# Gated linear attention and a soft mixture of experts: scores as sixteen 64x64 products, one DRAM row for k, q and v, more buffers, another order

## The chip, the core and the metric

The kernel runs on one core of a Trainium2 chip, in float32. The metric is the device time of one execution in microseconds. TensorE (PE) does the matrix products and transposes, with its weight loads shown as an engine of their own (PEld); VectorE (DVE), ScalarE (ACT) and GpSimd (POOL) do elementwise work; SyncE (SP) issues the DMAs.

## What is computed

Four batches of 768 tokens pass a linear attention of 8 heads of 48 columns with a gate per key column, and the result, 3072 tokens of 384 columns, passes a soft mixture of 8 experts with 4 slots each:

```python
f = 1 / (1 + exp(-f_logit))
for t in range(768):                                   # B=4, H=8, D=48
    state = f[:, :, t, :, None] * state + einsum('bhd,bhe->bhde', k[:, :, t], v[:, :, t])
    y[:, :, t] = einsum('bhd,bhde->bhe', q[:, :, t], state)
x = y.transpose(0, 2, 1, 3).reshape(3072, 384)
logits = x @ phi                                       # 384 x 32
d = softmax(logits, axis 0);  slot_input = d.T @ x
slot_out[e] = relu(slot_input[e] @ w1[e]) @ w2[e]      # 384 x 1024, 1024 x 384
out = softmax(logits, axis 1) @ slot_out
```

## The kernel before

**Blocks.** The attention is cut into 24 blocks of 128 tokens, six of each batch, in an order that walks the four batches side by side: block n belongs to batch n mod 4 and needs the state that block n-4 left. A block holds all eight heads as four pairs (a), each pair as two halves (r) of the 128 partitions, 48 rows used of 64. The two pairs of a bank are laid out in opposite directions of time, which is why masks and slices come mirrored.

In a block the gates come first: f is loaded (two blocks at a time), ACT takes exp and ln (L495, L498), DVE sums along time with two scans (L487, L488, with the tile `chain` of ones), and ACT takes exp of the sum and of its negative (L501, L502). Then k is multiplied by the one and q by the other (L524, L527, named mk and mq, on DVE or POOL). PE transposes k (L532, tk), a copy brings it from PSUM (L535, pk), PE forms k times v (L553, kv), and DVE adds the old state and scales it (L557, L562, sa and sm). For the output, PE multiplies q with the old state (L572, ie, not in the first four blocks), forms the scores of k with q (L541, sc), DVE multiplies them with a triangular mask (L544), PE multiplies them with v on top of the same bank (L581, ia), a copy brings the result to SBUF (L584, py), PE transposes it (L612, tx), and a copy makes it x (L615, px).

**Units.** After every fourth block a unit takes four blocks of x: logits (L630), running maximum, exponentials, their transposes (L651, L655), and a running sum of slot inputs (L659, L663). **The tail** after the last unit forms the slot inputs, runs the experts (first products L788 with twelve 1 MB tiles of w1, relu, transposes L803, second products L822 with twelve 1 MB tiles of w2), and combines and stores the output (L845, L854).

**The scores.** Each of a block's eight products takes 48 rows of k as weights, 128 columns wide, and streams 128 columns of q; the products of the two halves (r) use the two row halves of the array. The quarter of each 128x128 result that lies wholly above the diagonal is computed and masked out.

```python
for a in range(PR):
    for r in range(2):
        nc.tensor.matmul(ps[:, r, a], k_[rows[r], col(a)], queries(r, a), start=True, stop=True)
```

**What sets the order.** No order is written by hand. A class `Plan` takes every operation with its engine or choice of engines, the regions it reads and writes, a planned duration and a priority, and lists them greedily into one program order with a model of the engines. A table `LATER` shifts the priority of each kind of operation (eight numbers: blocks 0 to 3, then by block mod 4), a table `ENGINE` fixes the engine of a kind where there is a choice, and `WINDOW` says how near two starts must be for the priority to decide. The model counts a change of tile shape on PE, a page of 256 PE instructions to be fetched, and at most eight DMAs under way on SP's queue. Operations of POOL and those of DVE with two inputs in SBUF (scans, mk, mq) are made to exclude one another: each waits for the one before it in the program order. Each engine then runs its list strictly in order.

**Buffers.** k, q and v have rings of four blocks each (tiles ak, aq, av), scores two buffers (as), the gates three buffers of two blocks for f (af, ag) and two for the sums (ac). Of PSUM, one pair of banks (pr0) is the scores', two pairs (pr1, pr2) are y's, and two single banks (sg0, sg1) serve the rest. PE starts with 32 products of the tile `ones` with itself (L426), which warm it up; they wait for `ones` (L384), and DVE's first memsets clear banks (L403) and fill `chain` (L395).

Of the kernel before, what the change touches and what calls it, by code (L numbers as in the profile page):

```python
# [34 lines left out]
NHOME = 15  # L35
# [44 lines left out]
WINDOW = 0.21  # L80
LATER = {
# [1014 lines left out]
```

## Time and profile before

| | |
|---|---|
| median of 3 runs | 166.01 us (165.46 to 166.28) |
| the profiled execution | 165.66 us, of which the span from first to last instruction is 163.9 us |
| mean granted TensorE clock | 0.978 |
| PE busy | 146.5 us of the span (89%), 2461 matrix products |
| DVE busy | 120.2 us (73%) |
| ACT busy | 99.0 us (60%) |
| POOL busy | 26.3 us (16%) |
| DMA | 54.01 MB, 330 GB/s over the span |

The shares are averages over stages: a start up to about 28 us in which the first blocks' data arrive, the loop over the blocks up to about 113 us, the experts up to about 147 us, and the output. In the loop PE is busy nearly without a break, and DVE nearly so. A row of the chain of waits has a start, a duration and what ran then; rows of groups have a count, the busy time, the mean duration of one in ns, and the idle time of the engine before them with what ended it.

### The profile page before, as it was taken

The page shows a single profiled execution, that of the slowest core. Times are in us where ns is not written, and L with a number is a line of the kernel's source. Part 1 is how long each engine was busy: PE and PEld are TensorE (multiplying, and loading weights), DVE is VectorE, ACT ScalarE, POOL GpSimd, SP SyncE. Part 2 cuts the span into 40 slices and gives each one's busy share as a digit, 9 for nine tenths or more (in the row PEclk, how much of TensorE's full clock was granted, in tenths as well). Part 3 has the DMA queues.
Part 4 walks back from the last instruction along what each step waited for, and adds up shares of the span by engine and source line. Part 5 has one row for each costly group of instructions (what it writes and reads, how often), then busy time and mean ns, then how long its engine had stood idle before and what let it go on. Part 6 is the DMA issues. An engine that isn't in the chain of part 4 may idle for free.

```text
span 163.9 us, 5869 instructions
## 1 busy us (share of the span) xinstructions
PE 146.5 (89%) x2461; PEld 111.4 (68%) x2461; DVE 120.2 (73%) x234; ACT 99.0 (60%) x186; POOL 26.3 (16%) x43
## 2 busy tenths in 40 slices
PE   2978999999999999999999999999989999999500
PEld 2957777688777796788877887787852358677300
DVE  6789989899999999999999999999370133350400
ACT  4989987787869798873985876824430121033600
POOL 4002011050306030060308231250020000000000
PEclk9999999999999999999999999999999999999965
DMA  4999999999999899999999979529999996059491
GB/s 160 329 408 382 406 418 401 385 381 419 392 362 386 266 398 362 390 331 332 398 409 366 350 245 268 226 34 404 430 420 424 422 416 286 4 202 353 187 387 48
DMA packets 17603, 54.01 MB, mean 330 GB/s; under 512 B 1952, under 2 KB 5152, under 8 KB 14496
## 3 DMA queue, kind: packets, MB, share of 16 engines
q1 hardware_dynamic: 17568, 53.55, 86.2%
q8 instruction: 21, 0.34, 0.9%
q14 instruction: 14, 0.11, 0.2%
HBM read 48.82 MB, written 4.72 MB: 327 GB/s over the span
## 4 chain that ended last, share of the span: by engine, by line
PE 58%; DVE 13%; DMA 11%; ACT 9%; issue 3%; SPq 2%; POOL 1%; ACTq 0%; DVEq 0%; POOLq 0%
PE pr L541 10%; PE pr L581 6%; PE sg L612 5%; PE pr L788 5%; PE pr L572 5%; PE sg L822 5%; DMA av<-in_v_dram 5%; DMA ak<-in_k_dram 4%; DVE as L544 4%; PE sg L630 3%; PE pr L845 3%; PE sg L532 3%; PE sg L659 2%; DMA aq<-in_q_dram 2%; PE sg L553 2%
## 5 line engine op out<-in xcount | busy, mean ns | idle before, releaser
L544 DVE TENSOR_TENSOR as<-pr,tri 128x1024 f32<-128x1024 f32 x24 | 29.2, 1215 | 1.7 <-PE pr L541 1.0
L541 PE MATMUL pr<-aq,ak 48*128 48x128 f32 x384 | 27.9, 285 | 0.8 <-DVE ak L524 0.3
L541 PEld LDWEIGHTS pr<-aq,ak 48*128 48x128 f32 x384 | 23.3, 187 | 5.5 <-issue 2.4
L581 PE MATMUL pr<-as,av 128*48 128x128 f32 x384 | 24.1, 274 | 1.4 <-DVE as L544 1.2
L581 PEld LDWEIGHTS pr<-as,av 128*48 128x48 f32 x384 | 20.2, 123 | 3.0 <-DVE as L544 2.3
L612 PE MATMUL sg<-ident,xT 128*128 128x128 f32 x96 | 15.2, 282 | 0.4 <-ACT ag L535 0.2
L527 POOL TENSOR_TENSOR aq<-aq,ac 128x512 f32<-128x512 f32 x9 | 11.4, 1283 | 25.0 <-DMA aq<-in_q_dram 8.7
L584 ACT COPY xT<-pr 128x512 f32<-128x512 f32 x20 | 11.5, 582 | 5.5 <-PE pr L581 5.4
L524 POOL TENSOR_TENSOR ak<-ak,af 128x512 f32<-128x512 f32 x6 | 7.7, 1281 | 35.1 <-ACT af L501 23.4
L572 PE MATMUL pr<-aq,st 48*48 48x128 f32 x320 | 13.1, 279 | 0.2 <-DVE aq L527 0.2
L502 ACT ACTIVATE ac<-ac 128x1024 f32<-128x1024 f32 (+1 forms) x13 | 12.9, 993 | 0.5
L612 PEld LDWEIGHTS sg<-ident,xT 128*128 128x128 f32 x96 | 10.4, 141 | 3.6 <-issue 1.5
L532 PE MATMUL sg<-ident,ak 128*128 128x128 f32 x80 | 12.1, 282 | 0.2 <-DVE ak L524 0.2
L854 ACT COPY hm<-pr 128x768 f32<-128x768 f32 x7 | 5.5, 803 | 11.0 <-PE pr L845 11.0
L487 DVE TENSOR_TENSOR_SCAN ac<-chain,af 128x256 f32<-128x256 f32 x16 | 10.9, 683 | 1.1 <-issue 1.1
L535 ACT COPY ag<-sg 128x512 f32<-128x512 f32 x17 | 9.4, 585 | 3.6 <-PE sg L532 3.6
L615 ACT COPY xr<-sg 128x384 f32<-128x384 f32 x17 | 8.1, 480 | 4.9 <-PE sg L612 4.8
L488 DVE TENSOR_TENSOR_SCAN ac<-chain,af 128x256 f32<-128x256 f32 x16 | 10.7, 667 | 0.0
L553 PEld LDWEIGHTS sg<-av,ag 128*48 128x48 f32 x320 | 8.6, 124 | 2.7 <-issue 1.3
L527 DVE TENSOR_TENSOR aq<-aq,ac 128x512 f32<-128x512 f32 x15 | 10.2, 685 | 0.4 <-POOL ak L524 0.2
L572 PEld LDWEIGHTS pr<-aq,st 48*48 48x48 f32 x320 | 8.0, 119 | 3.4 <-issue 2.0
L532 PEld LDWEIGHTS sg<-ident,ak 128*128 128x128 f32 x80 | 8.5, 141 | 2.6 <-issue 0.9
(142 smaller groups left out, 240.7 us busy)
## 6 DMA issues: line engine op xcount, KB each, us to landing
hm<-in_w_dram SPq DMA_DIRECT2D x17, 1024.0 KB, 8.2
ak<-in_k_dram SPq DMA_DIRECT2D x24, 256.0 KB, 6.1
aq<-in_q_dram SPq DMA_DIRECT2D x24, 256.0 KB, 6.1
av<-in_v_dram SPq DMA_DIRECT2D x24, 192.0 KB, 5.6
out_dram<-hm SPq DMA_DIRECT2D x12, 384.0 KB, 3.8
af<-in_f_dram SPq DMA_DIRECT2D x7, 512.0 KB, 6.0
ag<-in_f_dram SPq DMA_DIRECT2D x4, 512.0 KB, 6.0
af<-in_w_dram SPq DMA_DIRECT2D x1, 1024.0 KB, 6.6
```

Source lines behind the costliest of these rows:

```text
L487: nc.vector.tensor_tensor_scan(cx[:, : 2 * BT], chain, lx[:, : 2 * BT], 0.0, op0=ALU.mult, op1=ALU.add)
L488: nc.vector.tensor_tensor_scan(cx[:, 2 * BT :][:, ::-1], chain, lx[:, 2 * BT :], 0.0, op0=ALU.mult, op1=ALU.add)
L502: add(f"p{n}", {"ACT": t_act(w)}, lambda e: nc.scalar.activation(flat(c_), flat(c_), AF.Exp, scale=-1.0), w=cs, prio=T(n, 1.2))
L527: tt(e)(flat(q_), flat(q_), flat(c_), op=ALU.mult)
L532: nc.tensor.transpose(pk[:, a], k_[:, a], ident)
L541: nc.tensor.matmul(ps[:, r, a], k_[rows[r], col(a)], queries(r, a), start=True, stop=True)
L544: tt(e)(sc_.rearrange("p r (m x) t -> p (r m) (x t)", x=2), bank(("sc", n)).rearrange("p r (m t) -> p (r m) t", m=2), tri.rearrange("p x t ...
L553: nc.tensor.matmul(pk[rows[r], col(a)], kp_[:, col(a), rows[r]], v_[:, 2 * a + r], start=True, stop=True)
L572: nc.tensor.matmul(py[at : at + D, r, a // 2], s0[rows[r], col(a)], queries(r, a), start=a < 2, stop=False, skip_group_check=True)
L581: nc.tensor.matmul(py[at : at + D, r, a // 2], v_[:, 2 * a + r], sc_[:, r, a], start=first and a < 2, stop=a >= 2, skip_group_check=True)
L584: copy(e)(xT[:, n % NXT].rearrange("p (r m) t -> p r (m t)", r=2), bank(("y", n))[:, :, : 2 * BT])
L612: nc.tensor.transpose(px[:, i], xT[:, n % NXT, i], ident)
```

## The change

**Scores.** A block's scores become sixteen products on the four 64x64 quadrants of the array (L588). For each pair and half, the 64 keys that all 128 queries may reach take 128 columns, and the other 64 keys only the 64 queries behind them. The skipped quarter of the bank is never written, so two memsets clear it at the start (L420).

**Inputs.** k, q and v of a block lie in one DRAM row of 1408 columns. Blocks 0 and 1 load three pieces, blocks 2 and 3 two (k with q, then v), the rest one; a ring of five blocks in one tile (ab) takes the place of ak, aq and av. The tiles of w1 are loaded in halves, spread over the blocks.

**Buffers.** Three score buffers, four for f, three for the sums; small tiles move to make room, and 13 tiles instead of 15 are kept for weights.

**Block 0.** Its gates and its products on k and q are done in two halves of two pairs.

**The order.** All numbers of `LATER`, the engines in `ENGINE`, `WINDOW` and some constants of the planner are new, the tail's groups stay the same, and the order of nearly everything moves. What each engine runs:

DVE at the start of the program, before: memsets, then the scans (L487, L488) and the products on q and k (L527, L524) of blocks 0 and 1, then block 0's mask (L544).

```order
L384 MEMSET ones 128x128
L409 COPY same<-ident 32x128 x4
L487 SCALAR_TENSOR_TENSOR ac<-chain,af 128x256
L488 SCALAR_TENSOR_TENSOR ac<-chain,af 128x256
L487 SCALAR_TENSOR_TENSOR ac<-chain,af 128x256
L488 SCALAR_TENSOR_TENSOR ac<-chain,af 128x256
L527 TENSOR_TENSOR aq<-aq,ac 128x512
L524 TENSOR_TENSOR ak<-ak,af 128x512
L527 TENSOR_TENSOR aq<-aq,ac 128x512
L524 TENSOR_TENSOR ak<-ak,af 128x512
L544 TENSOR_TENSOR as<-pr_62,tri 128x1024
```

(sg are the single banks, pr the pairs, ac and af tiles of the gates, tri the mask.) And now (st is a state), from the memset of `ones`, which stands behind those of pr0 and `chain`: block 0's halved scans (L522) and products (L571), the copy of its turned k (L579), its mask (L591), the scans of blocks 1 to 3 and block 0's state (L609), then block 1's product on k.

```order
L398 MEMSET ones 128x128
L426 COPY same<-ident 32x128 x4
L522 SCALAR_TENSOR_TENSOR ac<-chain,af 128x256 x2
L571 TENSOR_TENSOR ab<-ab,af 128x256 x2
L571 TENSOR_TENSOR ab<-ab,ac 128x256 x2
L579 COPY ag<-sg_65 128x512
L591 TENSOR_TENSOR as<-pr_62,tri 128x1024
L509 SCALAR_TENSOR_TENSOR ac<-chain,af 128x256
L510 SCALAR_TENSOR_TENSOR ac<-chain,af 128x256
L609 TENSOR_TENSOR st_86<-sg_66,ac 128x192
```

Block 1's products moved from before block 0's mask to behind it and behind six scans, and the copy of turned k, which ACT did, is now DVE's.

POOL from its triangular mask on, before: products on k (L524) and q (L527).

```order
L389 AFFINE_SELECT tri<-ones 128x128 x2
L524 TENSOR_TENSOR ak<-ak,af 128x512
L524 TENSOR_TENSOR ak<-ak,ag 128x512
L527 TENSOR_TENSOR aq<-aq,ac 128x512
L524 TENSOR_TENSOR ak<-ak,af 128x512 x2
```

And now (L571 is both products; those with ac or ae beside ab are q's of blocks 1 and 2, then of later ones):

```order
L403 AFFINE_SELECT tri<-ones 128x128 x2
L571 TENSOR_TENSOR ab<-ab,ac 128x512 x2
L534 COPY pend<-ac 128x8
L571 TENSOR_TENSOR ab<-ab,af 128x512
L571 TENSOR_TENSOR ab<-ab,ag 128x512 x2
L571 TENSOR_TENSOR ab<-ab,ae 128x512 x2
```

Up to block 4's mask POOL had two such products and has seven now; in the whole program it had 17 and has 27, and DVE has 12 fewer, with four halves added.

PE at the start, before: warming products, block 0's scores (L541), the transposes of k of blocks 0 and 1 (L532), block 0's scores with v (L581).

```order
L426 MATMUL sg_66<-ones 128x128 x16
L541 MATMUL pr_62<-aq,ak 128x128 x8
L532 MATMUL sg_65<-ident,ak 128x128 x4
L532 MATMUL sg_66<-ident,ak 128x128 x4
L581 MATMUL pr_63<-as,av 48x128 x8
```

And now, with block 0's transposes of k (L576) ahead of its scores (L588), which alternate two long and two short products:

```order
L443 MATMUL sg_66<-ones 128x128 x16
L576 MATMUL sg_65<-ident,ab 128x128 x4
L588 MATMUL pr_62<-ab 64x128 x2
L588 MATMUL pr_62<-ab 64x64 x2
L588 MATMUL pr_62<-ab 64x128 x2
```

The core of the diff:

```diff
-WINDOW = 0.21
+WINDOW = 0.09
 LATER = {
...
-    "mk": (20.3, 14, 24.2, 9.4, 17.6, -18.3, 17.3, -7.9), "mq": (7.6, -23.3, 11.9, -6.7, 16.8, 17.1, 12.7, 7),
+    "mask": (-13, 13, -25, -6.5, 0.3, 19.9, 7.7, 0.2), "mk": (19, 19.7, -9, 21.4, -7.1, 24.3, 15.4, 23.2),
+    "mq": (22.3, -14.3, -13.9, -21.2, 13.4, 19.8, -10.9, -6.5), "mx": (18, 21.3, -19.5, -19.3, -1.6, -0.9, -15, -15),
...
-    LAT, PE_LAT, SWITCH, DMA_LAT, RATE, DEPTH = 0.13, 0.17, 0.19, 2.0, 375e3, 8
-
-    INS, PAGE, FETCH = 4, 256, 5.8
+    LAT, PE_LAT, DMA_LAT, DEPTH = 0.13, 0.17, 2.0, 8
+
+    SWITCH = {"turn": 0.07, "col": 0.1, "row": 0.13, "slot": 0.16, "comb": 0.1, "sum": 0.1, None: 0.1}
+
+
+    INS, PAGE, FETCH, IDLE = 4, 256, 5.2, 3.6
...
-    NF, NK, NQ, NV, NSS, NXT = 3, 4, 4, 4, 5, 6
+    NF, NC, NB_, NSC, NSS, NXT = 4, 3, 5, 3, 5, 6
...
+    bb = [AB[:, ROW * i : ROW * i + ROW] for i in range(NB_)]
...
+        for x in range(2):
+            nc.vector.memset(pairs[0].rearrange("p r (m x t) -> p (r m) x t", m=2, x=2)[64 - 64 * x : 128 - 64 * x, :, x, :HT], 0.0)
...
-        load(kb[n % NK], k[n], f"k{n}", [("k", n % NK)], T(n, -9), 262144)
-        load(qb[n % NQ], q[n], f"q{n}", [("q", n % NQ)], T(n, -8.5), 262144)
-        load(vb[n % NV], v[n], f"v{n}", [("v", n % NV)], T(n, -7), 196608)
+        parts = ["kqv"] if n >= 4 else ["kq", "v"] if n >= 2 else ["k", "q", "v"]
+        for name in parts:
+            x = slice(512 * "kqv".index(name[0]), {"k": 512, "q": 1024, "v": ROW}[name[-1]])
+            load(bb[n % NB_][:, x], kqv[n, :, x], f"{name}{n}", [("b", n % NB_, c) for c in name], T(n, -7 if name == "v" else -8.5))
...
+        def half_gates(h, ex):
...
+            add(f"scan0.{h}", {"DVE": t_scan(256)}, scan_, two=True, r=[F_, sub(F_), C_, "chain"], w=[sub(C_)], prio=T(0, -1))
...
             for a in range(PR):
-                for r in range(2):
-                    nc.tensor.matmul(ps[:, r, a], k_[rows[r], col(a)], queries(r, a), start=True, stop=True)
+                for c in range(2):
+                    at = half[c ^ (a % 2)]
+                    for r in range(2):
+                        nc.tensor.matmul(ps[at, r, a, HT * c :], k_[rows[r], col(a), at], queries(r, a)[:, HT * c :], start=True, stop=True)
...
+                add(f"mk0.{h}", both, mul(k_, g_, at), two=True, r=[K, G, (*G, "half", h)], w=[HK[h]], prio=T(n, 2))
...
-        add(f"sc{n}", {"PE": 0.87}, scores, r=[K, Q, "kv0"], psum=("sc", n), kind=("sc",), prio=T(n, 4), after=ie, form="half", products=8)
+        add(f"sc{n}", {"PE": 0.67}, scores, r=[K, Q, *HK, *HQ, "kv0"], psum=("sc", n), kind=("sc",), prio=T(n, 4), after=ie, form="row", products=16)
...
+        for y, at in enumerate(halves):
+            if x < len(W1):
+                name, fn, key = f"w1{x}", load_w1(x, at), []
...
+            add(name, {"SP": 0.42}, fn, w=[("home", x), *key], prio=1e3 + 2 * x + y, dma=t_dma(HOME // 2), after=[paced[min(NN - 1, (2 * x + y) * 9 // 10)]])
```

More of the change, by code (lines that the diff above doesn't have):

```diff
@@ L34 @@
 HOME = 2048
-NHOME = 15
+ROW = 2 * PR * BT + DM
+NHOME = 13
 NX = 4
@@ L145, in __init__, with add @@
         self.bank = {}
-    def add(self, name, eng, fn, r=(), w=(), psum=None, kind=None, prio=0.0, bytes=0, after=(), two=False, form=None, products=0, ahead=0.0):
-        op = dict(name=name, eng=eng, fn=fn, psum=psum, kind=kind, prio=prio, bytes=bytes, n=len(self.ops), two=two, form=form, products=products, ahead=ahead)
+    def add(self, name, eng, fn, r=(), w=(), psum=None, kind=None, prio=0.0, dma=0.0, after=(), two=False, form=None, products=0, ahead=0.0):
+        op = dict(name=name, eng=eng, fn=fn, psum=psum, kind=kind, prio=prio, dma=dma, n=len(self.ops), two=two, form=form, sw=self.SWITCH[form], products=products, ahead=ahead)
         deps = set(after)
@@ L278, in gla_soft_moe_kernel @@
 @with_exitstack
-def gla_soft_moe_kernel(ctx: ExitStack, tc: tile.TileContext, q, k, f, v, fd, qd, kd, vd, phi, w1, w2, out):
+def gla_soft_moe_kernel(ctx: ExitStack, tc: tile.TileContext, f, kqv, fd, qd, kd, vd, phi, w1, w2, out):
     nc = tc.nc
@@ L587, in block @@
         paced.append(len(plan.ops))
-        add(f"mk{n}", both, mul_k, two=True, r=[G], w=[K], prio=T(n, 2))
-        add(f"mq{n}", both, mul_q, two=True, r=[CB], w=[Q], prio=T(n, 2.1))
+        HK, HQ, HC = ([(*k, "half", h) for h in range(2)] if n == 0 else [] for k in (K, Q, CB))
+        if n:
+            add(f"mk{n}", both, mul(k_, g_), two=True, r=[G], w=[K], prio=T(n, 2))
+            add(f"mq{n}", both, mul(q_, c_), two=True, r=[CB], w=[Q], prio=T(n, 2.1))
+        else:
+            both = {"POOL": t_pool(256), "DVE": t_dve(256)}
+            for h in range(2):
+                at = slice(2 * h, 2 * h + 2)
+                add(f"mk0.{h}", both, mul(k_, g_, at), two=True, r=[K, G, (*G, "half", h)], w=[HK[h]], prio=T(n, 2))
+                add(f"mq0.{h}", both, mul(q_, c_, at), two=True, r=[Q, CB, HC[h]], w=[HQ[h]], prio=T(n, 2.1))
         if not final:
-            add(f"tk{n}", {"PE": 0.4}, turn_k, r=[K, "ident"], psum=("kt", n), kind=("one",), prio=T(n, 3), form="turn", products=4)
+            add(f"tk{n}", {"PE": 0.48}, turn_k, r=[K, *HK, "ident"], psum=("kt", n), kind=("one",), prio=T(n, 3), form="turn", products=2)
             add(f"pk{n}", {"ACT": t_act(512), "DVE": t_dve(512, True)}, put_k, psum=("kt", n), w=[KP], prio=T(n, 3.5))
@@ L681, in unit @@
         for w_ in (1, 0):
-            add(f"te{u}", {"PE": 0.11}, tr(w_), r=[("et", "lt")[w_], "ident"], psum=("el", u, w_), kind=("one",), prio=t0 + 0.6 - 0.1 * w_, form="turn", products=1)
-            add(f"pe{u}", {"ACT": 0.28, "DVE": 0.25}, put_e(w_), psum=("el", u, w_), w=[(("el",), ("ltok", u))[w_]], prio=t0 + 0.8)
-        add(f"pi{u}", {"PE": 0.42}, pins, r=[("el",), *[("x", (n0 + g) % NX) for g in range(UB)]], psum=("pi", u), kind=("one",), prio=t0 + 1, form="slot", products=4)
+            kind = ("e", "l")[w_]
+            add(f"t{kind}{u}", {"PE": 0.2}, tr(w_), r=[("et", "lt")[w_], "ident"], psum=("el", u, w_), kind=("one",), prio=t0 + 0.6 - 0.1 * w_, form="turn", products=0.5)
+            add(f"p{kind}{u}", {"ACT": 0.28, "DVE": 0.25}, put_e(w_), psum=("el", u, w_), w=[(("el",), ("ltok", u))[w_]], prio=t0 + 0.8)
+        add(f"pi{u}", {"PE": 0.62}, pins, r=[("el",), *[("x", (n0 + g) % NX) for g in range(UB)]], psum=("pi", u), kind=("one",), prio=t0 + 1, form="slot", products=4)
         add(f"pp{u}", {"DVE": t_dve(384, True)}, put_p, r=[AL] if u else [], psum=("pi", u), w=["pin"], prio=t0 + 1.2)
@@ L739, in fill @@
         def fill(e):
-            nc.tensor.matmul(bank("fill")[:, :128], ones, ones, start=True, stop=True)
+            nc.tensor.matmul(bank("fill")[:, :128], ident, ident, start=True, stop=True)
         def t_wb(e):
@@ L773, in tail @@
         for x in range(4):
-            add(f"fill{x}", {"PE": 0.2}, fill, r=["ones"], w=[("bank", "fill")] if x else [], psum="fill", kind=None if x else ("spare",), prio=t0 + 50, form="sum", products=1, after=[last])
+            add(f"fill{x}", {"PE": 0.2}, fill, r=["ident"], w=[("bank", "fill")] if x else [], psum="fill", kind=None if x else ("spare",), prio=t0 + 50, form="sum", products=1, after=[last])
         add("twb", {"ACT": 0.2}, t_wb, r=["zr1", ("nm", L)], w=["wb"], prio=t0)
-        add("twd", {"DVE": 0.15}, t_wd, r=["wb", "same"], w=["wd"], prio=t0)
+        add("twd", {"DVE": 0.15}, t_wd, r=["wb", "same"], w=["wd", "tri"], prio=t0)
         add("psi", {"PE": 0.21}, psi, r=["wd", "pin"], psum="psi", kind=("one",), prio=t0, form="slot", products=12)
@@ L922, in gla_soft_moe_kernel @@
         slots(th)
+    add("flag1", {"DVE": 2.6}, flag1, r=["esum", ("es", 0), ("es", 1), "si"], w=[("pend", n) for n in range(NN)], prio=T(NN, 20))
+    add("flag2", {"PE": 0.15}, flag2, r=[("pend", 0), "ident"], psum="flag", kind=("one",), prio=T(NN, 20), products=1)
+    add("flag3", {"DVE": 0.6}, flag3, psum="flag", w=["flag"], prio=T(NN, 20))
     spots = list(ARENA.values()) + [(homes[x], [("home", x)]) for x in range(len(W1))]
@@ L972, in gla_soft_moe_kernel @@
     PW = DP + D
-    py, sel = pairs[1], homes[7][:, : 2 * 176].rearrange("p (x c) -> p x c", x=2)
+    py, sel = pairs[1], homes[6][:, : 2 * 176].rearrange("p (x c) -> p x c", x=2)
     NE2 = 2
-    turned = [homes[8 + i // 4][:, 512 * (i % 4) : 512 * (i % 4) + 512].rearrange("p (i t) -> p i t", i=PR) for i in range(NN)]
+    turned = [homes[7 + i // 4][:, 512 * (i % 4) : 512 * (i % 4) + 512].rearrange("p (i t) -> p i t", i=PR) for i in range(NN)]
     def general_pair(b, p):
@@ L1028, in general @@
         for o in plan.order:
-            if o["n"] >= ending:
+            if o["n"] >= ending and o["name"] not in ("flag1", "flag2", "flag3"):
                 o["fn"](o["on"])
```

152 lines of the change are left out of this document (87 added, 65 removed), and 67 rows, old and new, of the table LATER.

## The prediction

> **What bounds the kernel now.** I read the busy table by windows first, then the chain of waits in order of time, then the groups by line and shape, then the timeline of the start. In a window row the columns are the window, its length, then busy us and count of PE, PE's weight loads, DVE, ACT and POOL, the granted clock, the DMA share and GB/s.
>
> ```profile
> 9.00:18.75 9.75, 8.12 (x117) 6.45 (x117) 8.80 (x15) 8.98 (x16) 1.28 (x1) 1.00 1.06 399
> 18.75:30.00 11.25, 10.84 (x190) 8.79 (x194) 10.19 (x17) 8.22 (x17) 1.27 (x1) 1.00 1.02 404
> 30.00:45.00 15.00, 14.78 (x276) 11.88 (x270) 13.93 (x25) 12.90 (x21) 3.80 (x3) 1.00 1.03 394
> 45.00:60.00 15.00, 15.00 (x280) 12.14 (x276) 14.47 (x26) 11.95 (x23) 2.57 (x3) 1.00 0.97 351
> 60.00:75.00 15.00, 14.73 (x258) 11.81 (x254) 14.45 (x30) 11.34 (x22) 3.76 (x3) 1.00 0.99 364
> 75.00:90.00 15.00, 14.80 (x261) 11.87 (x262) 14.69 (x27) 11.33 (x23) 4.46 (x5) 1.00 1.00 376
> 90.00:105.00 15.00, 14.82 (x277) 12.03 (x272) 14.35 (x29) 11.52 (x24) 3.70 (x12) 1.00 0.88 293
> ```
>
> From 30 to 105 us PE is busy 74.1 of 75 us at full clock, so PE bounds the block loop. DVE is right beside it: 71.9 of 75, which leaves it 3.1 us idle. ACT has a fifth free, POOL three quarters. A saving on PE alone is therefore worth only what DVE can follow, and the sum needs both engines.
>
> The chain of waits (start us, us, what) gives what each PE group costs from its start to the next group's start:
>
> ```profile
> 28.29 1.09 PE pr L541 x16
> 66.76 0.58 PE pr L572 x16
> 67.34 0.59 PE sg L532 x4
> 67.93 0.44 PE sg L612 x4
> 70.24 0.49 PE sg L553 x16
> 70.73 1.75 PE pr L581 x32
> 77.81 0.85 PE sg L553 x32
> 89.46 0.88 PE pr L581 x16
> 112.01 1.12 PE pr L541 x16
> 113.15 1.24 DVE as L544
> 122.74 7.05 PE pr L788 x64
> ```
>
> I number blocks 0 to 23. Block 4's scores (L541) start at 28.29 and block 23's at 112.01, 83.7 us apart; block 23's mask (L544 at 113.15) opens the last stretch, which leads to the first expert product (L788 at 122.74).
>
> **The scores on PE.** Eight products of 128 columns, two at a time in the array, are replaced by sixteen on four quadrants; each quadrant streams 2x128+2x64 = 384 columns, against 512 on each of the two halves before. A second group of L581 adds 1.75−0.88 = 0.87 us for 8 products of 128 columns, two at a time (4 steps of 0.218, or 0.109 for each of the two passes that the records show). L572, eight products on four quadrants, costs 0.58 = 4 passes x 0.109 + 0.144. The new group has 6 passes per quadrant: 6x0.109+0.15 = 0.80, an estimate. No row shows this group. Nearest below is L572's 0.58, nearest above the old group's 1.09; a second price by records is 0.36/16 = 22.5 ns each (0.85−0.49 for L553), with 32 records 0.87. I take 0.80, since L572 has the same tile. That is 0.29 less per block.
>
> ```profile
> 37.65 0.33 PE L572 MATMUL pr<-aq,st 48*48 48x128 f32 x4
> ```
>
> The Trainium skill, page "TensorE: Matmul & The Clock Gate", section "Wait — 56ns, not 53.3ns?", states that matmuls never start closer than about 25 ns, however short; by it the group would be 32x0.025+0.155 = 0.955, an estimate from that page. The trace's 22.5 ns a record on L553 lies slightly below that figure.
>
> Fewer changes of tile shape come with it: scores and the products on the old state (L572) now have one shape, and in the order on PE the changes fall from 113 to 105. One change costs 0.13 to 0.15 (L553 alone 0.49, following another 0.36; a transpose group 0.59, following another 0.44), so 8x0.14 = 1.1. From block 4's scores to block 23's stand 19 score groups: 19x0.29+1.1 = 6.6. PE would take 83.7−6.6 = 77.1 us.
>
> **DVE in the same stretch** (mask of block 4 to mask of block 23).
>
> ```profile
> L527 POOL TENSOR_TENSOR aq<-aq,ac 128x512 f32<-128x512 f32 x9 | 11.4, 1283 | 25.0 <-DMA aq<-in_q_dram 8.7 <-DMA av<-in_v_dram 7.3 <-DVE xr L615 7.2
> L527 DVE TENSOR_TENSOR aq<-aq,ac 128x512 f32<-128x512 f32 x15 | 10.2, 685 | 0.4 <-POOL ak L524 0.2
> L535 DVE COPY ag<-sg 128x512 f32<-128x512 f32 x3 | 2.0, 682 | 0.0
> L584 DVE COPY xT<-pr 128x512 f32<-128x512 f32 x4 | 2.7, 685 | 0.9 <-PE pr L581 0.9
> L615 DVE COPY xr<-sg 128x384 f32<-128x384 f32 x7 | 3.9, 551 | 0.1
> L655 DVE COPY ltok<-sg 128x128 f32<-128x128 f32 x1 | 0.3, 292 | 0.0
> 30.03 1.20 DVE L544 TENSOR_TENSOR as<-pr,tri 128x1024 f32<-128x1024 f32 x1
> ```
>
> By the order, k and q products there go from 21 to 16 (−5x0.685 = −3.4), copies of y from 3 to none (−2.1), copies of the turned k from 3 to 4 (+0.7), of x from 5 to 4 (−0.6), small 128x128 copies from 1 to 6 (+1.5), and the five checks on flags, one 128x256 product and one state sum leave (about −1.7): −5.6 us of durations. DVE's rows overlap, a scan of 0.67 starts 0.60 after the one before, so they count about 0.9 of that: −5.0. ACT takes the copies; it has 3 us in 15 free. POOL takes the products at 1.283 each. From mask to mask DVE takes 113.15−30.03 = 83.1 now and 78.1 then.
>
> **The start**, rows of the timeline (start us, us, engine, line):
>
> ```profile
> 3.11 5.46 PE L426 MATMUL sg<-ones 128*128 128x128 f32 x32 [3.11 <-DVE ones L384]
> 8.91 1.16 PE L541 MATMUL pr<-aq,ak 48*128 48x128 f32 x16 [0.34 <-DVE ak L524]
> 10.68 1.22 DVE L544 TENSOR_TENSOR as<-pr,tri 128x1024 f32<-128x1024 f32 x1
> 11.82 0.68 DVE L487 TENSOR_TENSOR_SCAN ac<-chain,af 128x256 f32<-128x256 f32 x1
> 12.42 0.67 DVE L488 TENSOR_TENSOR_SCAN ac<-chain,af 128x256 f32<-128x256 f32 x1
> 13.68 1.16 PE L541 MATMUL pr<-aq,ak 48*128 48x128 f32 x16
> 15.48 1.28 POOL L524 TENSOR_TENSOR ak<-ak,af 128x512 f32<-128x512 f32 x1 [11.74 <-DMA aq<-in_q_dram]
> ```
>
> The two added memsets of the score bank and those of `chain` now stand ahead of `ones`, on which the 32 warming matmuls wait: they move from 3.11 to about 3.7 and end near 9.1. Block 0's halved gates and products are done by about 7.8, but the next DVE instruction is the copy of block 0's turned k, and its transpose stands behind the warming matmuls. DVE waits some 2 us there. Block 0's mask comes at about 10.6, as before (10.68), but block 1's products, done by then before, now stand behind six scans (3.6 us) and a state product: block 1's scores move from 13.68 to about 17.7, with 1.28 us of POOL's q product in that path. Then POOL's q product of block 2 (to 19.8), block 2's scores at 20, POOL's k product of block 3 (22.1 to 23.4), block 3's scores at 25.5. POOL's four products of blocks 4 and 5 run from 26.0 on; the third, block 4's q, ends at 26.0+3x1.28 = 29.9, then L572's successor (0.58) and block 4's scores at about **30.6, 2.4 us later** than 28.22. These times are my replay from durations. Bounds: nothing (the wait is filled) and 4.0 (block 1's delay is kept whole). I take 2.4 for PE and the mask alike. I cost the loads at nothing: they carry the same bytes in fewer rows, and in my replay each block's data land before its products' turn. The cover is thin, since the windows show the DMA engines full up to 45 us; gone, it would cost what the start's upper bound allows.
>
> **The sum.** PE: block 23's scores at 30.6+77.1 = 107.7, 4.3 earlier. DVE: block 23's mask at 32.4+78.1 = 110.5, 2.6 earlier. The later sets the end, but part of DVE's 3.1 idle us was waiting for PE's scores and goes with PE's gain; a fifth of it is 0.6, so **3.2 earlier**. The last stretch, experts and output, has the same groups, and I cost its new order at nothing, plus or minus 0.3. The profiled run took 165.66, of which 163.9 is its span; it lies 0.35 below the median of 166.01. 165.66−3.2 = **162.4**. More buffers (5 for k, q, v, 3 for scores) I cost at nothing: no wait in the loop's chain ends on them before. Code fetch is also left at nothing:
>
> ```profile
> q8 instruction: 21, 0.34, 0.9%
> ```
>
> PE's instructions per block rise by a fifth, and this queue's 21 packets take 0.009x16x163.9/21 = 1.1 us each; no PE group of the loop shows a pause inside now. If some came late PE would wait about that long for each, and the range's upper part covers three such waits.
>
> **Rivals.**
> *The start isn't later* (another engine's work fills DVE's wait; block 4 at 28.22): only PE's 6.6 counts with DVE following, 159.1. For it: POOL and ACT are nearly idle in the first 20 us. Against: the DVE order is fixed, and the scans stand behind that wait.
> *A record has a least price, however short.* By the first L553 group, 0.49/16 = 30.6 ns, the 32 records take 0.98, saving 0.11: 19x0.11+1.1 = 3.2 on PE, block 23's scores at 30.6+80.5 = 111.1, 0.9 earlier: 164.8. Against: a second L553 group has 22.5. The page named above says the same of its 25 ns, and by it the group saves 0.135.
> *The quadrants don't run free*, so that the change doesn't do what it says. If a 64-column product must end no earlier than the 128-column one issued beside it, a group has 8 passes, 8x0.109+0.15 = 1.02, saving 0.07: 19x0.07+1.1 = 2.4, block 23's scores at 111.9, as before: 165.6. Against: the four products of the 37.65 row lie within 0.33 us, thus overlapped. The Trainium skill, same page, section "The mechanism" of Part 3, states that matmuls start and end in program order; here long and short alternate in pairs, so by it the times would be those of this rival if each short one waited. The traces don't show mixed lengths.
> *Slower: POOL holds up DVE.* Products on POOL and two-input work on DVE exclude one another in the program's order. In the groups above DVE's k and q products waited only 0.2 us for POOL, with 15 such products on POOL in this stretch; it has 20 then. DVE's work is 83.1−3.4 (its idle share) −5.0 = 74.7; at 0.5 us for each, block 23's mask comes at 32.4+74.7+10 = 117.1, 3.9 later: 169.6. It makes the kernel slower by 0.5% from (113.15+1.15−32.4−74.7)/20 = 0.36 us each. For it: 1.28 against 0.69 us, and DVE at 96%. Against: DVE has copies from PSUM, which need no exclusion, to put beside them.
>
> **Chances.** Forecast (160.5 to 164.5) 0.52; start not later 0.15; least price 0.08; quadrants bound 0.10; POOL 0.10; a mixture ending near the old time 0.05. Half a per cent, 0.8 us, is about what a measurement of this kernel can tell from no change. Faster: 0.52+0.15+0.08 = 0.75. Same: the quadrants' case and most of the mixture, 0.13; slower 0.12. The range goes from 158.0, a microsecond under the first rival, to 166.2, which leaves out POOL's case and the edges.
>
> **What would show it.** The score group's step in the chain: 0.80 (0.98 and 1.02 are the rivals'). Block 4's scores near 30.6 and a DVE wait of about 2 us before the copy of turned k at 8 to 10 us. In the loop, DVE's idle time by releaser: POOL under 0.2 us each. From block 4's scores to block 23's 77 to 79 us. From the first expert product to the end 41.2 as now. I am wrong if PE shows waits inside the score group, or if the loop's idle time on PE rises above 4 us.

## The result and the profile after

| | before | changed |
|---|---|---|
| median | 165.5 us (165.25 to 166.28, 6 runs) | 173.96 us (173.21 to 177.12, 6 runs) |
| ratio, 95% interval | 1 | 1.047 (1.044 to 1.050) |
| span of the profiled run | 163.9 us | 175.4 us |
| block 4's scores | 28.2 | 33.1 |
| block 23's scores | 111.9 | 122.6 |

The change makes the kernel 4.7% slower; 162.4 had been forecast. The profiled run of the changed kernel took 177.1 us: the granted clock fell in its loop and, to go by its mean (0.937 in both), in one more of the six, and the ratio is from the other four (173.2 to 174.4). In the two profiles the span grows by 11.5 us: 4.9 until block 4's scores start, 5.7 from there to block 23's, 0.9 behind them. The loop takes 89.5 us so. The half clock stands in it for 6.8 us, which is at most 3.4 us of lost work, so without it the loop would take 86 us or more, an estimate.

"Block 23's scores" stands here, as in the prediction, for the last of the 24 score groups. In the order before that is a group of an even block (in e4, where odd blocks alone have the new products, it has 16 records and not 32), so it is block 22's; both stretches hold 19 groups all the same.

Block 4's scores in the changed kernel:

```profile
33.09 0.40 PE L588 MATMUL pr<-ab 48*64 48x128 f32 x10
```

The windows of the changed kernel, columns as before:

```profile
9.00:18.75 9.75, 6.20 (x86) 4.91 (x85) 6.32 (x11) 6.33 (x11) 1.12 (x1) 0.90 1.03 394
18.75:30.00 11.25, 10.15 (x193) 8.72 (x194) 9.56 (x15) 9.47 (x15) 4.24 (x6) 0.79 0.80 292
30.00:45.00 15.00, 13.90 (x304) 10.82 (x305) 12.02 (x23) 11.56 (x22) 6.08 (x5) 1.00 1.00 387
45.00:60.00 15.00, 13.91 (x313) 11.32 (x311) 13.53 (x25) 10.84 (x19) 5.03 (x4) 1.00 0.97 361
60.00:75.00 15.00, 13.81 (x310) 11.39 (x309) 13.82 (x27) 12.74 (x25) 5.80 (x5) 1.00 0.90 332
75.00:90.00 15.00, 13.98 (x298) 10.89 (x300) 12.59 (x25) 10.57 (x22) 6.28 (x5) 1.00 0.99 352
90.00:105.00 15.00, 13.19 (x251) 10.11 (x243) 10.70 (x21) 8.90 (x19) 1.92 (x3) 0.77 0.61 209
```

PE was busy 14.7 to 15.0 of every 15 us of the loop; now it is busy 13.2 to 14.0, DVE has more idle time too, and so has ACT in all windows of the loop but one: no engine is full. In the start the clock column shows 0.90 and 0.79 where it was 1.00, and again 0.77 from 90 us on.

What PE waits for between block 4's and block 23's scores (waits of PE in that window: us in total, times, longest):

```profile
PE pr L628 <- issue: 1.8, 1, 1.8
PE pr L588 <- issue: 1.5, 3, 0.9
PE sg L667 <- issue: 1.2, 1, 1.2
PE sg L706 <- DVE lt L689: 1.0, 1, 1.0
PE pr L619 <- issue: 0.9, 1, 0.9
PE pr L588 <- DVE as L591: 0.5, 1, 0.5
```

5.4 us end with "issue": no semaphore, no engine, no DMA of data that the profile shows. The timeline of PE shows where they stand:

```profile
37.08 0.66 PE L588 MATMUL pr<-ab 48*64 48x128 f32 x17
38.63 0.56 PE L588 MATMUL pr<-ab 48*64 48x128 f32 x15 [0.90 <-issue]
56.85 0.38 PE L588 MATMUL pr<-ab 48*64 48x128 f32 x7 [0.40 <-issue]
61.94 0.27 PE L667 MATMUL sg<-ident,xT 128*128 128x128 f32 x1
63.41 0.49 PE L667 MATMUL sg<-ident,xT 128*128 128x128 f32 x3 [1.19 <-issue]
94.95 0.84 PE L628 MATMUL pr<-as,ab 128*48 128x128 f32 x8 [1.81 <-issue]
```

They cut a group of the same operation in two, one of them after the first of four transposes, where nothing new is to be waited for. Counted from the start of the program, the long steps in the middle of a group come after matmul records 473, 600, 854, 981, 1236, 1363 and 1618: 127 or 128 records apart, or two or three times that. A record goes with a weight load, so 127 records are 254 instructions. And on the queue of instruction packets (q8), 16 KB each, the ones from 36.3 to 92.8 us start 5.97 to 6.6 us apart; before the change six of the eleven distances in the loop were 7.2 to 7.7. At 38.63 PE goes on 1.4 us after a packet that began at 36.26 and took 1.0 us.

It does so each time. From 38.6 to 95.0 us PE passes ten such ends of a page (every 127th or 128th record), and at all ten the next record starts 1.2 to 1.6 us after the last packet has ended. The packet behind it begins 3.5 to 4.3 us after PE has passed the end of a page, at nine of the ten. These two and the 0.9 to 1.1 us of the packet itself make up the 6 us. It looks as if a page were asked for only when PE enters the one before it; the profile doesn't show the asking.

The Trainium skill, page "Runtime: NRT & Kernel Launch", section "Instruction fetch mechanics", states that an engine's code is fetched in blocks of 16 KiB, 256 instructions, while it runs, and that this is mostly hidden. The trace agrees on the size. It was hidden before the change, and it isn't after it.

The chain of waits has the groups' own steps, and the start:

```profile
3.84 6.73 PE sg L443 x32
10.57 0.44 PE sg L576 x4
60.74 0.67 PE pr L588 x22
84.26 0.81 PE pr L588 x24
95.80 1.48 PE pr L588 x24
122.62 0.81 PE pr L588 x24
132.50 7.07 PE pr L844 x64
```

A score group takes 0.81, and 0.67 between two groups of L619, which has the same shape; 0.80 had been forecast. At half clock it takes 1.48. The warming products end at 10.57 instead of 8.6: they start 0.7 later, and the full clock came at 9.9 instead of 6.5 us. DVE waits behind them, for the transposes of block 0's k:

```profile
11.04 0.69 DVE L579 COPY ag<-sg 128x512 f32<-128x512 f32 x1 [2.84 <-PE sg L576]
```

### The profile page after: what moved, and what is told of

The parts are those of the page before. It is cut to its first block, busy times and chain, and to the rows that moved or that the text cites. A ratio compares the mean times of both kernels' runs of the same rounds, so it can differ in the third digit from the quotient of the medians.

```text
span 175.4 us, 6545 instructions
## 1 busy us (share of the span) xinstructions
PE 147.2 (84%) x2845; PEld 112.5 (64%) x2845; DVE 118.1 (67%) x230; ACT 97.6 (56%) x187; POOL 39.6 (23%) x55
## 4 chain that ended last, share of the span: by engine, by line
PE 67%; DVE 15%; issue 8%; POOL 2%; ACT 2%; DVEq 0%; POOLq 0%; ACTq 0%
PE pr L628 10%; PE pr L588 9%; PE sg L667 6%; PE sg L576 5%; PE pr L619 5%; PE pr L844 5%; PE sg L878 4%; PE sg L443 4%; PE sg L685 3%; PE sg L600 3%; PE pr L901 3%; PE sg L714 2%; PE pr L878 2%; POOL ab L571 2%; DVE ac L509 2%
## 5 line engine op out<-in xcount | busy, mean ns | idle before, releaser
L588 PE MATMUL pr<-ab 48*64 48x128 f32 (+1 forms) x768 | 24.1, 263 | 2.3 <-issue 1.5
L588 PEld LDWEIGHTS pr<-ab 48*64 48x64 f32 x768 | 20.9, 144 | 6.4 <-issue 3.3
L591 DVE TENSOR_TENSOR as<-pr,tri 128x1024 f32<-128x1024 f32 x16 | 19.4, 1212 | 3.0 <-PE pr L588 3.0
L571 POOL TENSOR_TENSOR ab<-ab,ac 128x512 f32<-128x512 f32 x10 | 12.9, 1294 | 30.7 <-DVE ab L571 20.8
L628 PE MATMUL pr<-as,ab 128*48 128x128 f32 x256 | 17.3, 277 | 2.7 <-issue 1.8
L628 PEld LDWEIGHTS pr<-as,ab 128*48 128x48 f32 x256 | 13.3, 123 | 4.5 <-issue 2.6
L667 PEld LDWEIGHTS sg<-ident,xT 128*128 128x128 f32 x96 | 10.6, 144 | 8.3 <-issue 3.9
L619 PE MATMUL pr<-ab,st 48*48 48x128 f32 x320 | 13.8, 283 | 0.9 <-issue 0.9
L576 PE MATMUL sg<-ident,ab 128*128 128x128 f32 x80 | 13.6, 302 | 0.9 <-DVE ab L571 0.7
L591 DVE TENSOR_TENSOR ab<-pr,tri 128x1024 f32<-128x1024 f32 x8 | 9.8, 1220 | 4.4 <-PE pr L588 4.1
L576 PEld LDWEIGHTS sg<-ident,ab 128*128 128x128 f32 x80 | 9.7, 152 | 2.8 <-DVE ab L571 1.0
L619 PEld LDWEIGHTS pr<-ab,st 48*48 48x48 f32 x320 | 8.8, 122 | 3.3 <-issue 2.8
L600 PE MATMUL sg<-ab,ag 128*48 128x48 f32 x320 | 10.8, 214 | 0.0
L571 POOL TENSOR_TENSOR ab<-ab,ag 128x512 f32<-128x512 f32 x6 | 7.7, 1284 | 12.3 <-PE sg L714 7.5
L579 ACT COPY ag<-sg 128x512 f32<-128x512 f32 x13 | 7.6, 583 | 3.4 <-PE sg L576 3.3
L571 POOL TENSOR_TENSOR ab<-ab,af 128x512 f32<-128x512 f32 x5 | 6.4, 1279 | 13.5 <-ACT af L548 10.4
```

What stands on the lines that cost most here:

```text
L571: return lambda e: tt(e)(flat(x[:, at]), flat(x[:, at]), flat(y[:, at]), op=ALU.mult)
L576: nc.tensor.transpose(pk[:, a], k_[:, a], ident)
L588: nc.tensor.matmul(ps[at, r, a, HT * c :], k_[rows[r], col(a), at], queries(r, a)[:, HT * c :], start=True, stop=True)
L591: tt(e)(sc_.rearrange("p r (m x) t -> p (r m) (x t)", x=2), bank(("sc", n)).rearrange("p r (m t) -> p (r m) t", m=2), tri.rearrange("p x t ...
L600: nc.tensor.matmul(pk[rows[r], col(a)], kp_[:, col(a), rows[r]], v_[:, 2 * a + r], start=True, stop=True)
L619: nc.tensor.matmul(py[at : at + D, r, a // 2], s0[rows[r], col(a)], queries(r, a), start=a < 2, stop=False, skip_group_check=True)
```

## The experiments

A is the theory that PE's code pages come too slowly for the sixteen products, B that the start and order alone cost the time. "Products" in the expectations' distances are the records that the profile counts, two for each product. "Loop" is from block 4's to block 23's scores, 83.7 us before and 89.5 in the changed kernel.

**e1: the changed kernel with the old products.** Nothing but the lines of `scores`:

```diff
-                for c in range(2):
-                    at = half[c ^ (a % 2)]
-                    for r in range(2):
-                        nc.tensor.matmul(ps[at, r, a, HT * c :], k_[rows[r], col(a), at], queries(r, a)[:, HT * c :], start=True, stop=True)
+                for r in range(2):
+                    nc.tensor.matmul(ps[:, r, a], k_[rows[r], col(a)], queries(r, a), start=True, stop=True)
```

> The changed kernel with block scores again as eight products of 128 columns, all else as changed. Theory A (code supply): PE's code comes in packets of 16 KB on queue q8, the smallest distances between packets in the changed loop are about 6.0 us, and pauses without a visible releaser stand 127 products apart; with 165 instead of 197 PE instructions a block the pauses go, blocks 4 to 23 take 82 to 85 us instead of 89.5, and the time falls to 168 to 171 us. Theory B (start and order alone cost the time, the sixteen products are a gain of 0.29 us a block): the time rises by about 5 us, to 177 to 180. Under A what stays above 165.5 is the start, block 4's scores near 32 us instead of 28.2.

173.87 us (ratio 1.048, 1.045 to 1.052); the profiled run, 172.24, is the fastest of the five. PE in its timeline, block 4 and block 23:

```profile
33.37 0.38 PE L586 MATMUL pr<-ab 48*128 48x128 f32 x2
118.69 0.38 PE L586 MATMUL pr<-ab 48*128 48x128 f32 x2
```

The pauses are gone and the loop takes 85.3, as A said; but the time stays what it was with the sixteen products, against both. The start, 33.4 instead of 28.2, is no matter of the products. In the changed kernel the sixteen products are worth nothing in the end: what they save on PE goes where the pauses are. And the new order by itself, with the old products, is no gain in the loop either: 85.3 against the 83.7 of the old order.

**e2: the kernel before with the new products.** The same diff the other way round, and the two memsets of the bank stand behind the copies into `same`.

> The kernel before, with its own order, engines, loads and buffers; only the scores become sixteen quadrant products (and two memsets clear the skipped quarter). A: the loop's 19 blocks from block 4's scores to block 23's need 19x197/256 = 14.6 pages of code at 6.05 us, 88.5 us instead of 83.7; pauses 127 products apart; 168 to 171 us. B: the start is the old one, so the scores' gain shows: 160 to 162 us.

Its four runs took 166.41, 167.59, 170.45 and 170.51 us, the kernel before 165.27 to 166.79 beside them. The profile is of the second. The start is the old one, 28.0; the loop takes 86.0 instead of 83.7, between A and what the fewer columns would give. Block 4's and block 23's scores:

```profile
28.00 0.40 PE L546 MATMUL pr<-aq,ak 48*64 48x128 f32 x10
114.00 0.33 PE L546 MATMUL pr<-aq,ak 48*64 48x128 f32 x4 [0.31 <-DVE as L549]
```

The chain shows the pauses again:

```profile
55.17 0.48 PE sg L617 x3
55.65 1.29 issue
56.95 0.27 PE sg L617
57.22 0.58 PE pr L577 x16
57.80 1.78 PE sg L535 x8
```

Behind this pause of 1.29 us, between the third and the fourth transpose of a group, the clock fell for 3.4 us: the eight transposes of L535 take 1.78 instead of 1.02. So the sixteen products alone, with the old start, bring none of B's 160 to 162 us, and in this profile they cost 2.3 us of loop. That the kernel as a whole gets slower by them isn't shown: the fastest run lies among those of the kernel before, and two are below A's 168 to 171.

**e3: the instructions alone.** The old products, each cut into two of 64 columns:

```diff
-                    nc.tensor.matmul(ps[:, r, a], k_[rows[r], col(a)], queries(r, a), start=True, stop=True)
+                    for c in range(2):
+                        nc.tensor.matmul(ps[:, r, a, HT * c : HT * c + HT], k_[rows[r], col(a)], queries(r, a)[:, HT * c : HT * c + HT], start=True, stop=True)
```

(in the kernel the loop over c stands outside that over r).

> The kernel before, with each of the eight score products cut into two of 64 columns in the same two row halves: as many PE instructions as the sixteen quadrant products, no column less. It measures the price of the instructions alone. A: 168 to 171 us, pauses 127 products apart, packets on q8 about 6.0 us apart. B: the array work is the same, 165 to 167 us, no pauses.

184.27 us (ratio 1.110, 1.106 to 1.114): far above both. No pause for code is left, because PE is slow in another way:

```profile
L542 PE MATMUL pr<-aq,ak 48*128 48x64 f32 x768 | 48.0, 275 | 0.2 <-DVE as L545 0.2
L542 PEld LDWEIGHTS pr<-aq,ak 48*128 48x128 f32 x768 | 44.7, 188 | 4.8 <-issue 3.9 <-DVE as L545 0.5 <-DVE ak L524 0.2
```

The group takes 1.93 us instead of 1.09: 32 records with weights of 128 columns cost 60 ns each with 64 columns behind them, where 16 with 128 columns behind them cost 68. The run doesn't tell A from B. It tells that fewer columns alone gain nothing: the halves of the keys, 64 columns of weights on quadrants, belong to the gain.

**e4 and e7: half the blocks.** In e4 the kernel before, with e2's memsets, has the new products in odd blocks (`if n % 2`), the old ones in even blocks; e7 adds:

```diff
+    for o in plan.order:
+        if o["on"] == "DVE" and re.fullmatch(r"p[ky]([4-9]|1[0-9]|2[0-3])", o["name"]):
+            o["on"] = "ACT"
```

> The kernel before with the quadrant products in odd blocks alone. A: 19x181/256 = 13.4 pages at 6.05 us are 81 us, no longer above PE's own work of about 81, so few pauses: 162.5 to 165.5 us. B: half the gain of all blocks, 163 to 164.

> The kernel before with quadrant products in odd blocks, and DVE's seven copies of y and of turned k of blocks 4 on moved to ACT: DVE has 7x0.685 = 4.8 us less. If DVE was what kept the odd-block version at 165.5, the time is 162.5 to 164.5; if PE's code and the waits between engines kept it, it stays at 165 to 166.

e4: 165.48 us, ratio 0.997 (0.994 to 0.9998), the fastest version, by 0.3%, at the edge of the noise. Its loop takes 83.1, with one pause of 0.6 us. e7: 166.18, ratio 0.999 (0.996 to 1.003), loop 83.9. The 4.8 us taken off DVE bring nothing, so DVE's busy time isn't what kept e4 (though ACT got the copies).

**e6, e16, e11, e12: the weights' traffic.** All weight loads of the loop are moved behind the last block's loads (in SP's order; the same operations):

```diff
+    late = [o for o in plan.order if o["on"] == "SP" and re.match(r"w[12]", o["name"])][: 2 * NHOME]
+    rest_ = [o for o in plan.order if not any(o is x for x in late)]
+    at_ = [x for x, o in enumerate(rest_) if o["name"] == "kqv23"][0] + 1
+    plan.order = rest_[:at_] + late + rest_[at_:]
```

e6 is the changed kernel so, e16 the same with the old products, e11 is e2 so, and e12 the kernel before so. In e11 and e12 one load of v also comes behind the weights, and two weight tiles land in buffers of the gates before their last use; their last blocks wait and have other values, so they are read up to block 19 only.

> The changed kernel with all weight loads of the loop issued only behind the last block's row of k, q and v: the loop has about 230 GB/s instead of 350 to 390, and the experts then wait for their weights, so the total is longer (180 to 195 us) and only the loop is read. Theory A1 (a code page waits on its way behind the block's data): packets on q8 can follow each other in under 5 us, the pauses 127 products apart go, and blocks 4 to 23 take 77 to 82 us as forecast instead of 89.5. Rival A2 (a page costs its 6 us whatever else moves): the pauses and 86 to 90 us stay. Rival A3 (DVE or POOL holds the loop): pauses go, and the loop still takes 84 us or more.

> The changed kernel with eight products for the scores (as e1) and all weight loads of the loop behind the last block's row (as e6): the control of e6 in the changed order; only the loop is read. Theory A1 (traffic matters through the code pages alone): blocks 4 to 23 take 84 to 86 us, as e1's 85.3, so that e6's 82.2 against it is what the sixteen products are worth in this order without late pages, 2 to 4 us and not the 6.6 that PE's work falls. Rival (less traffic helps the loop otherwise): 83 or less.

> The kernel before with the sixteen products alone (as e2), and all weight loads of the loop behind the last block's loads; only the loop is read, as the experts wait for their weights (180 to 200 us). Theory A1 (pages come late because of the traffic): blocks 4 to 23 take 77 to 81 us instead of 86.0, no clock drop in the loop. Rival: 85 to 87.

> The kernel before, unchanged but for the weight loads of the loop, which stand behind the last block's loads: the control of e11 and of the late weights in the changed kernel. A1: PE isn't short of code there, so the loop stays within 1 us of 83.7 and the traffic alone is no gain. Rival (lower traffic speeds the loop in other ways, by earlier data for instance): 82 us or less, and then e11's gain isn't the pages'.

The totals (192.4, 198.1, 203.8 and 208.1 us) hold the wait for weights. PE in the timelines, block 4 and block 23 of e6, then of e16:

```profile
32.06 0.51 PE L588 MATMUL pr<-ab 48*64 48x128 f32 x14
114.22 0.44 PE L588 MATMUL pr<-ab 48*64 48x128 f32 x8
```

```profile
33.99 0.38 PE L586 MATMUL pr<-ab 48*128 48x128 f32 x2
119.17 0.38 PE L586 MATMUL pr<-ab 48*128 48x128 f32 x2
```

and block 4 and block 19 of e11, then of e12:

```profile
27.76 0.40 PE L546 MATMUL pr<-aq,ak 48*64 48x128 f32 x10
93.22 0.43 PE L546 MATMUL pr<-aq,ak 48*64 48x128 f32 x8 [0.32 <-DVE as L549]
```

```profile
28.49 0.38 PE L541 MATMUL pr<-aq,ak 48*128 48x128 f32 x2
95.64 0.38 PE L541 MATMUL pr<-aq,ak 48*128 48x128 f32 x2
```

| | full traffic | weights late |
|---|---|---|
| changed order, old products, loop | 85.3 (e1) | 85.2 (e16) |
| changed order, new products, loop | 89.5 | 82.2 (e6) |
| old order, old products, blocks 4 to 19 | 67.2 | 67.2 (e12) |
| old order, new products, blocks 4 to 19 | 69.8 (e2) | 65.5 (e11) |

Two windows of e6, to be held against 361 and 352 GB/s of the changed kernel:

```profile
45.00:60.00 15.00, 14.86 (x354) 12.37 (x346) 14.25 (x28) 11.54 (x26) 4.30 (x4) 1.00 0.65 216
75.00:90.00 15.00, 13.74 (x334) 11.01 (x334) 14.02 (x27) 12.36 (x23) 5.05 (x5) 1.00 0.54 183
```

With the old products the traffic makes no difference at all, in either order; with the new ones it makes 7.3 and 4.3 us. So A1 holds, though e6's 82.2 lies just above its 77 to 82: the code pages come late because of the data that move beside them, and only the kernel with more instructions needs them sooner. At the ten page ends at which the changed kernel stood right behind a packet, e6 is 2.0 to 4.3 us behind it at six, and 1.3 to 1.4 at the other four. The half clock from 95.3 to 102.1 us, at most 3.4 us of lost work, is part of the 7.3, and e2's of 3.4 us, at most 1.7, of the 4.3: each follows a pause, and neither e6's nor e11's loop has one (a pause of 1.3 us and one of 0.2 are left in e6). Without them the traffic makes some 4 us in the changed order and 2.6 in the old one, as an estimate at the least. Once pages are in time the new products are worth 3.0 and 1.7 us, not the 6.6 of PE's work.

**e8: the changed kernel again.**

> The changed kernel once more, for a profile that no clock drop in the loop disturbs. Theory A: pauses 127 products apart again, 4 to 7 us of them between block 4's and block 23's scores, block 4's scores at 32 to 33.5 us, 173 to 174.5 us.

176.23 and 171.83 us. Its profile shows the clock drop again at 95.3, behind a pause after the same record 1618; block 4 starts at 33.1, the loop takes 88.9. No profile of the changed kernel is without the drop.

**e5, e13, e9: the start.** e5 halves the warming, e13 adds spare products to it, e9 moves POOL's early products in e5 to DVE.

```diff
-        return lambda e: [nc.tensor.matmul(ones_[1][:, :128], ones, ones, start=True, stop=True) for _ in range(2)]
+        return lambda e: [nc.tensor.matmul(ones_[1][:, :128], ones, ones, start=True, stop=True)]
...
+    put_behind("ia0", spare(12))
+    put_behind("tx0", spare(4))
...
+        if o["on"] == "POOL" and re.fullmatch(r"m[kq][1-5]", o["name"]):
+            o["on"] = "DVE"
```

> The changed kernel with half the warming products (16 instead of 32 records). Theory S (the start is late because block 0's transposes, scores and mask stand behind the warming products, and the load of phi behind them too): block 0's transposes move from 10.6 to about 7.6, block 4's scores from about 33 to 30.5, and the time falls by about 2.5 us, to 171 to 172. Rival S2 (the start is late by the products on POOL and the order of scans): block 4's scores stay within 1 us of 33, and the time stays at 173 to 174. If the clock is granted later for want of warming, the start is no earlier either, and the clock row shows it.

> The changed kernel with half the warming products (e5), and 16 products of the identity with itself into an unused part of a bank, twelve behind block 0's L628 and four behind its transposes of x, where PE idles. Theory C (the rest of the late start is the half clock that follows PE's idle time, granted from 15.5 to 22.3 us in e5): the clock stays full from the first grant on, block 4's scores come at 29 to 30 instead of 31.2. Rival O (the order: block 1's gates stand behind block 0's scores and mask): the clock may stay full, and block 4's scores stay within 0.7 us of 31.2.

> The changed kernel with half the warming products and POOL's seven products of blocks 1 to 5 on DVE instead. Half the warming alone brought block 4's scores from 33.1 to 31.2. Theory P (the rest of the late start is POOL's slower products, 1.28 us against 0.69, and the handing over between POOL and DVE): block 4's scores come at 28 to 29.5, and the time is 169 to 172 us. Rival (the rest is the order of DVE's scans and masks, which seven more products lengthen): block 4's scores stay at 30.5 or later.

Block 4's scores in e5, e13 and e9, in this order:

```profile
31.16 0.40 PE L588 MATMUL pr<-ab 48*64 48x128 f32 x10
```

```profile
30.27 0.40 PE L588 MATMUL pr<-ab 48*64 48x128 f32 x10
```

```profile
30.86 0.40 PE L588 MATMUL pr<-ab 48*64 48x128 f32 x10
```

Half the warming brings 1.9 of the 4.9 us (e5 took 172.4 to 178.2 us in four runs; its profile has two clock drops in the loop). The window from 18.75 to 30 us shows what e13 does to the clock, e5 first:

```profile
18.75:30.00 11.25, 10.35 (x182) 8.65 (x180) 8.48 (x14) 9.01 (x17) 4.65 (x5) 0.84 0.93 348
```

```profile
18.75:30.00 11.25, 9.42 (x203) 7.77 (x202) 9.01 (x15) 10.44 (x19) 6.15 (x7) 1.00 1.02 396
```

Full clock throughout brings 0.9 more, between the two theories' ranges (30.27, where C has 29 to 30 and O 30.5 or later; e13 took 170.1 and 175.5 us in its two runs). Moving POOL's seven products brings 0.3: theory P falls. Steps as small as these are within the scatter of single profiles: with one order of the start, block 4's scores come at 33.1 in the changed kernel and in e8, at 32.1 in e6 and at 34.0 in e16; and in e10 (below), which is e9 with fewer new products, they come at 32.2 instead of 30.9, and the half clock lasts until 24.4 us instead of 20.8.

**e14, e15, e10: order and combinations.** e14 gives block 1 its old place in e5's start; e15 and e10 are e14 and e9 with the new products in odd blocks only.

```diff
+    put_at("f0", 1, take(["f1"]))
+    put_at("q0", 1, take(["k1", "q1"]))
+    moved = take(["exp1", "ln1", "scan1", "g1", "p1", "mk1", "mq1"])
+    moved[-1]["on"] = "DVE"
+    put_at("pk0", 0, moved)
+    put_at("sm0", 1, take(["tk1", "sc1", "mask1"]))
```

> The kernel of e5 with block 1's part of the start in the old place: f of block 1 loaded second, k and q of block 1 behind those of block 0, its gates and products (on DVE) ahead of block 0's copy of turned k, its transposes, scores and mask behind block 0's state. Theory O: block 1's scores come at 12.5 to 14.5 instead of 16.5, block 4's at 28 to 29.5, and the time falls to 169 to 172 us. Rival C (the clock): block 4's scores stay at 30.5 or later, with the clock at half in 14 to 22 us.

> The kernel of e14 with quadrant products in odd blocks alone. If start and code pages are the two causes, both are now near the old state: block 4's scores as in e14, the loop 83 to 85 us, 165 to 168.5 us in all. If a third cause keeps the loop, as its 84.7 us in e10 hints, it stays at 168 or above.

> The kernel of the run e9 with quadrant products in odd blocks alone. Theory A (code pages bound the changed loop): pauses 127 products apart shrink to under 2 us in the loop, blocks 4 to 23 take 82 to 84 us instead of about 89, so this version is 2 to 4 us faster than e9 although PE's own work is 3 us more. Rival (the pauses are not the loop's bound): it is as fast as e9 or slower.

e14: 183.04 us, block 4 at 36.8. Block 1's products were done by 11.9, but its scores stayed at 16.6, behind block 0's kv and L628 at half clock, and its mask then kept DVE from the scans of blocks 2 and 3:

```profile
18.12 1.23 DVE L591 TENSOR_TENSOR as<-pr,tri 128x1024 f32<-128x1024 f32 x1 [4.25 <-PE pr L588]
```

It made the start worse and doesn't tell whether the order is the rest. e15: 176.47, far above the 168.5 that start and pages were to give, for its start is as late as e14's (37.7); its loop is 84.3 against e14's 92.5. e10: 169.3, 171.1, 171.3 and 177.0 us against e9's 171.2, 173.4, 176.6 and 176.8, with a loop of 84.7 instead of 88.5 (of which a clock drop of 3.4 us may have cost 1.7). As A has it, the version with half the new products isn't slower but faster, although PE works more. Start and pages explain most of the loss as far as stages can be added, since e15's and e10's loops are back at 84 to 85; no run has both mended in the changed kernel.

## Why the prediction was wrong

**What held.** The score group's 0.80 (0.81, and 0.67 between groups of L619). PE's own work: with every group at its shortest step behind the same kind of group, the 19 blocks take 81.4 us before and 74.7 in e6, 6.7 less, where 6.6 was forecast (sorted by the group that follows, 82.0 and 76.7, 5.3 less). Of the rivals, a least price per record (0.98) and quadrants that wait for one another (1.02) are refuted by the step. The Trainium skill, page "TensorE: Matmul & The Clock Gate", section "Wait — 56ns, not 53.3ns?", has 25 ns between the starts of matmuls at the least. That isn't met: 0.67 us for 32 records are 21 ns each, and the measurement decides. Refuted too is POOL holding up DVE, which waited for POOL 0.3 us in all. Two of the signs that the prediction names for being wrong came: PE waits inside the score group (at 38.63), and from 30 to 105 us it is idle for 6.2 us, not under 4.

**The step that failed** is "Code fetch is also left at nothing". The instructions per block were known to rise by a fifth, and the reason given, that no PE group of the loop shows a pause now, says only that pages were in time at one per some 7 us. The changed kernel's trace has 1778 matmul records in the loop, 14.0 pages of 127 (the expectations count 14.6). At the forecast's pace of 77.1 us one was needed every 5.5 us, and under the loop's traffic they came 6.0 to 6.6 us apart, 6.3 in the mean: 14 of them take 84 us at the least of these and 88 at the mean, an estimate. 5.4 us of pauses and, behind the longest, a half clock of 6.8 us (3.4 us of lost work at most) took back the gain in the profiled run; e6 and e11 win some of it by lighter traffic, and with fewer instructions the pauses go (e1) or nearly go (e4). The range covered three waits of a microsecond. The warning stood in the diff: the planner of the changed kernel lets a page of 256 PE instructions take 5.2 us while loads are under way and 3.6 otherwise (FETCH and IDLE; 5.8 before), which leaves next to nothing against 5.5 and is less than the runs show.

**The second, a size.** The start was forecast 2.4 us later and came 4.9 later. The order of events was the forecast one (DVE waits 2.8 us for the transposes behind the warming products), but the warming ended at 10.6 instead of 9.1, for the full clock came 3.4 us later, and the clock then fell while PE waited. Of the 4.9, half the warming accounts for 1.9, and, each tried alone on top of it and no larger than the scatter, the clock for 0.9 and POOL's products for 0.3. The other 1.8 us are open; the order of blocks 1 to 3 is the likeliest cause and wasn't shown.

**The third.** PE's saving was taken to be worth what DVE follows, up to 3.2 us with the late start, thus 5.6 in the loop. With pages in time it is worth 3.0 in this order and 1.7 over 15 blocks in the old one; against the kernel before, e6's loop is 1.5 shorter. By the first of the two counts above, e6 has 7.5 us in its loop in which PE doesn't work at its shortest step, against 2.3 before; 1.5 of them are pauses for pages still. e7 shows that DVE's busy time isn't the reason; which waits between engines take the rest wasn't settled.

**Behind the loop** the span is 0.9 longer; 0.3 had been allowed. From the first expert product (132.50) to the end it takes 42.9 us, not the 41.2 of before. In e1, with the same order behind the loop, the part behind it takes 51.8 us, as in the kernel before (51.9), so the 0.9 isn't shown to come from the order; its cause stays open.

## What to carry to other kernels

More and smaller matmuls can be cheaper in array time and still lose, because PE's code is a stream that must arrive: before the gain is counted, hold the time in which PE will use up a packet of instructions after the change against the time between packets under the same traffic. Pauses that end with "issue" in the middle of a group, at equal distances in instructions, are the mark of late code, and fewer instructions or less traffic are two ways to test it. A new order has to be priced at the start as well: there PE's idle time came back as half clock (0.79 in the mean from 18.75 to 30 us, 0.84 in e5, and 1.00 in e13, where spare products fill the idle time).

## What the hardware showed that was not expected

- One code page of 16 KB lasts 127 matmul records with their weight loads. With 330 to 390 GB/s beside them, they came 5.97 to 6.6 us apart in the changed loop from 36 to 93 us. Closer packets are there too: one at 96.0 us, 3.2 behind the last, and one before the change, 4.0 behind. Which engine's code a packet holds isn't shown.
- The granted clock changed 6.83 us apart in the start (9.93, 16.75, 23.58 us), and it fell behind a single pause of 1.8 us of PE in the loop, and of 1.3 in e2. It did not behind one of 1.2 (63.4 us), of 1.3 in e6 or of 1.6 in e7. The Trainium skill, page "TensorE: Matmul & The Clock Gate", section "What's actually happening", has a free-running window of 3.4 us. The steps here are two of them, and in e2 one.
- Products of 64 columns with weights of 128 cost 60 ns a record (e3), those with weights of 64 on four quadrants 0.67/32 = 21 ns.
